# Middle projection ahead of the forward transform, 16-bit sine angles, merged product instructions, a partly moved bonus, free PSUM banks and a new written order in a two-layer RWKV-6 / Hyena kernel

## The chip, the cores and the metric

One core of one Trainium2 chip runs the whole program. The metric is device time in microseconds (us), the median of several executions. A profile of one execution accompanies it; its span is counted from the first to the last profiled event, and the time of an execution is a little longer than its span.

Five instruction queues work side by side, each strictly in its own order: PE (TensorE, matmuls; its weight loads are shown as PEld), DVE (VectorE), ACT (ScalarE), POOL (GpSimd) and SP (SyncE, which issues most DMA transfers). An instruction that waits for another queue holds up everything behind it in its own queue.

## The reference

Two layers follow one another. The first is a linear recurrence with a decaying state (batch 4, 8 heads, 768 steps, 48 wide); the second projects its output three ways, convolves the middle projection with a filter by a Fourier transform, gates it with the two others and projects it out.

```python
for t in range(S):
    cur = np.einsum('bhd,bhe->bhde', u[None] * kt, vt)
    y[:, :, t] = np.einsum('bhd,bhde->bhe', rt, state + cur)
    state = wt[:, :, :, None] * state + np.einsum('bhd,bhe->bhde', kt, vt)
...
x = attn_out.transpose(0, 2, 1, 3).reshape(B, S, H * D)
proj = x @ w_proj
x1, x2, x3 = (proj[..., :D], proj[..., D:2 * D], proj[..., 2 * D:])
X2 = np.fft.rfft(x2, n=S, axis=1)
H = np.fft.rfft(filter_fft, n=S, axis=0)[None, :, :]
x2_conv = np.fft.irfft(X2 * H, n=S, axis=1)
y = x1 * x2_conv * x3
return y @ w_out
```

Everything arrives and leaves in float32; matmuls run on bf16 operands. In the second layer the width is 384.

## The kernel before

**First layer.** The 768 steps of each batch are six chunks of 128, 24 chunks in all (0 to 5 are batch 0, and so on). Chunks are loaded in groups: {0}, {1}, {2, 3}, {4, 5} and then pairs. Every chunk has four loads of 192 KB (lw, lk, lr, lv), issued by SP. For a chunk the steps are, by the names in the written order:

- ln (ACT): logarithm of w; cs (PE): its running sums, as two 128x384 matmuls and four tiny ones; ex (ACT): exponentials; kq (DVE): k and r scaled by them; ph (ACT): the decay of the whole chunk.
- tr (PE) turns kq, qk (ACT or DVE) copies the turned tile out of PSUM, sc (PE) forms the 128x128 scores of eight heads, mt (DVE, or ACT followed by mc on POOL) masks them, half of the heads at a time.
- rk, ru, rh, cc (POOL and DVE) form the bonus r.(u*k), vb is v in bf16, vc (mostly POOL) is v times the bonus. yi (PE) adds vc into the chunk's output through an identity matmul of two 128x192 pieces.
- ki, kv (PE) and su (DVE) carry the state; ys (PE) applies it; y (PE) applies the masked scores; xn copies the output to SBUF; yt (PE) turns it and xT copies that.

**Second layer.** For each batch, `second(b)` describes:

- gates: p (PE) and cp (ACT or DVE) give x1; q and cq (DVE) multiply by x3. Together they need wproj0 and wproj2.
- the middle path: sd (DVE, POOL) folds the two halves of xn into sum and difference; z (PE) applies the forward transform table F to them; cz copies; f (PE) applies the middle projection; cf copies into X.
- products: U0 to U3 and P0, P1 multiply X by the filter's spectrum (HR, HI, HG).
- inverse: E (PE) with tables mi and mx, cE (ACT) copies one half, aE (DVE) adds and subtracts, dE (DVE, POOL) folds, yE multiplies by the gate; o (PE), co and so are the output projection, copy and store.

The filter's spectrum is made once, between (filt, fsd, h, hc, hg). The tables F, mi and mx are sines: DVE writes angles as 32-bit integers (ang, ia) and masks them to 16 bits (L1465, L1511), ACT takes the sine (sin, is0, is1). Sine, and the logarithm and exponential, need different activation tables; each change of table is a load on ACT.

**Order.** Nothing is scheduled automatically. A long string lists every step with its engine (P, A, D, G, S, or "-" for a step that is left out) and, for PE, the PSUM bank it writes; a trailing name ties a POOL step behind a DVE step. Each queue gets its instructions in exactly this order. `warm n b` puts n matmuls without a use into PE's queue. PSUM's eight banks are three pairs and two singles. k, r, v and w have three load slots each, one slot per group, so that group 3 reuses the slot of group 0.

Of the kernel before, what the change touches and what calls it, by code (L numbers as in the profile page):

```python
# [12 lines left out]
INT32 = mybir.dt.int32  # L13
AF = mybir.ActivationFunctionType
# [21 lines left out]
NLD, NG, NF, NS, NX, NO = 3, 2, 4, 3, 5, 5  # L36
NP = 3
# [4 lines left out]
smalls D  # L42
maps G
lw0 S
kz2 D
kz0 D
u S
kz3 D
kz1 D
xz D  # L50
lk0 S
imaps G
pads D
lr0 S
lv0 S
masks G
ur A
lw1 S
um P 3
lk1 S  # L60
ub A
lr1 S
ang0 D
lv1 S
vb0 A
ia2 D
lw2 S
sin0 A
ia1 D
lk2 S  # L70
ia0 D
lr2 S
lv2 S
iw D
vb1 A
ang2 D
lw3 S
is0 A
is1 A
lk3 S  # L80
ang1 D
sin2 A
lr3 S
rk0 D
lv3 S
sin1 A
rk1 D
ru0 D
table A
ru1 D  # L90
rh0 D
rh1 G ru1
cc0 D
vc0 G ru1
cc1 D
ln0 A
ln1 A
lw4 S
warm 27 1
cs0 P 0  # L100
vc1 D
cs1 P 1
rk2 D
ex0 A
ex1 A
kq0 D
vb2 G rk2
ln2 A
kq1 D
ru2 G rk2  # L110
lk4 S
warm 7 2
tr0 P 4
ph0 A
lr4 S
cs2 P 2
qk0 D
ph1 A
lv4 S
kv0 P 3  # L120
ex2 A
cs3 P 0
lw5 S
su0 D
rh2 G rk2
sc0 P 1
lk5 S
ex3 A
kq2 D
tr1 P 4  # L130
ki1 P 3
mt0.0 A
kv1 P
qk1 D
ph2 A
mt0.1 A
mc0.0 G rk2
tr2 P 2
lr5 S
kq3 D  # L140
sc1 P 1
mc0.1 G rk2
mt1.1 A
lv5 S
qk2 D
tr3 P 4
ph3 A
mt1.0 D
mc1.0 -
mc1.1 G rk2  # L150
yi0 P 0
qk3 A
y0 P
lw6 S
sc2 P 2
cc2 D
yi1 P 1
su1 D
ys1 P
mt2.1 A  # L160
lk6 S
vc2 G rk2
y1 P
xn0 D
ki2 P 4
ln3 A
kv2 P
mt2.0 D
mc2.0 -
sc3 P 0  # L170
lr6 S
yt0 P 3
xn1 A
su2 D
cs4 P 2
mt3.1 D
mc3.1 -
mc2.1 G rk2
xT0 A
yi2 P 1  # L180
lv6 S
ex4 A
ys2 P
mt3.0 D
mc3.0 -
rk3 G rk2
y2 P
yt1 P 4
ki3 P 3
xn2 A  # L190
xT1 D
cs5 P 0
lw7 S
kq4 D
yi3 P 1
yt2 P 4
ex5 A
kv3 P
lk7 S
vb3 G rk2  # L200
ys3 P
su3 D
y3 P
ph4 A
xT2 A
kq5 D
tr4 P 2
xn3 A
lr7 S
ki4 P 3  # L210
qk4 A
wproj0 G kq5
yt3 P 4
ru3 D
kv4 P
sd3.1 D
tr5 P 1
filt S
su4 D
xT3 A  # L220
rh3 G ru3
sc4 P 2
qk5 D
ph5 A
mt4.1 A
lv7 S
sd3.0 G ru3
cc3 D
warm 2 3
sc5 P 0  # L230
ln4 A
mt4.0 D
mc4.0 -
lw8 S
vc3 G ru3
mt5.1 D
mc5.1 -
warm 3 3
cs6 P 1
cs7 P 2  # L240
mt5.0 D
mc5.0 -
ex6 A
mc4.1 G ru3
yi4 P 0
ex7 A
kq6 D
ys4 P
y4 P
xn4 A  # L250
warm 2 4
tr6 P 3
ph6 A
sd4.1 D
lk8 S
sd4.0 D
yi5 P 0
yt4 P 4
qk6 A
kq7 D  # L260
rk4 G sd4.1
ys5 P
y5 P
lr8 S
p0.0.0 P 1
xT4 A
xn5 A
tr7 P 3
ph7 A
cp0.0.0 A  # L270
sd5.0 D
yt5 P 4
sd5.1 D
sc6 P 0
ru4 G sd5.0
xT5 D
qk7 A
p0.2.0 P 2
mt6.1 D
mc6.1 -  # L280
z0.2 P 1
mt6.0 D
mc6.0 -
cp0.2.0 A
rh4 D
p0.2.1 P 4
cz0.2 A
fsd0 D
lv8 S
sc7 P 2  # L290
z0.0 P 0
cp0.2.1 A
vb4 A
lw9 S
cc4 D
p0.0.1 P 1
cz0.0 A
fsd1 D
lk9 S
z0.1 P 0  # L300
cp0.0.1 A
lr9 S
mt7.1 D
mc7.1 -
wproj1 G fsd1
h0 P 1
cz0.1 A
mt7.0 D
mc7.0 -
lv9 S  # L310
vc4 G cc4
h1 P 2
hc0 A
lw10 S
ln5 A
kv6 P 3
hg0 D
h2 P 0
lk10 S
hc1 A  # L320
su6 D
ki7 P 4
yi6 P 1
hc2 A
y6 P
hg1 D
cs8 P 2
wproj2 G hg1
xn6 D
# [1486 lines left out]
```

## Time and profile before

| what | value |
|---|---|
| time, median of 3 runs | 159.8 us (159.7 to 160.09) |
| profiled execution, span | 159.0 us |
| HBM read, written | 22.41 MB, 4.72 MB |
| mean DMA rate over the span | 165 GB/s |
| load of w, k, r or v: 192 KB, issue to landing | 3.8 to 4.0 us (24 of each) |
| filter load, 1152 KB | 8.7 us |
| wproj loads, three of 288 KB (POOL queue) | 5.6 us |
| store of 384 KB / 192 KB | 2.7 / 1.9 us |

The span is shorter than the time by the launch and the end of the program. In the profile an "L" number is a line of the kernel; a helper's line (L1194 multiplies, L1198 and L1200 copies) stands for many steps, so steps are told apart by the tiles they write. "idle before" with an arrow names what ended the idle time of an engine. A slice of the page's second part is a fortieth of the span, and its digits are busy tenths. A window row gives busy time, with the number of instructions in brackets.

### The profile page before, as it was taken

What the parts mean: (1) busy time and instruction counts of PE and PEld (TensorE: products, weight loads), DVE (VectorE), ACT (ScalarE), POOL (GpSimd) and SP (SyncE); (2) the same over time, 40 slices, a digit from 0 to 9 for tenths busy, and PEclk for the clock granted to TensorE, in tenths of its full rate; (3) what the DMA queues carried; (4) which work ended last, traced back from release to release, by engine and by line L of the source; (5) the groups of instructions that cost most, each with busy time, mean ns of one, the idle gap of its engine ahead of it and who ended that gap; (6) DMA issues with size and microseconds to landing.
All of it is one profiled execution on the core that took longest, in us unless ns stands there. A gap on an engine that the chain in (4) does not pass through costs nothing.

```text
span 159.0 us, 4355 instructions
## 1 busy us (share of the span) xinstructions
PE 143.1 (90%) x1674; PEld 92.0 (58%) x1675; DVE 139.4 (88%) x289; ACT 126.6 (80%) x218; POOL 92.7 (58%) x98
## 2 busy tenths in 40 slices
PE   0990798998999999999999999999999999999880
PEld 0340366755656766757666777676677667666530
DVE  7992559988894999999999999999998999999980
ACT  4469848987889985999989989999988967775631
POOL 7411535976715166999957899879688823200400
PEclk9998579999999999999999999999999999999999
DMA  4999488999999999799998899989800004203136
GB/s 85 226 219 221 91 170 160 203 179 288 246 194 188 232 202 203 138 173 211 209 214 177 174 222 200 190 157 265 258 0 4 0 35 173 93 2 139 63 149 247
DMA packets 104118, 26.23 MB, mean 165 GB/s; under 512 B 100129, under 2 KB 102690, under 8 KB 104098
## 3 DMA queue, kind: packets, MB, share of 16 engines
q1 hardware_dynamic: 102498, 24.78, 70.4%
q0 software_dynamic: 1600, 1.18, 5.4%
q8 instruction: 13, 0.21, 0.6%
q14 instruction: 7, 0.06, 0.1%
HBM read 22.41 MB, written 4.72 MB: 171 GB/s over the span
## 4 chain that ended last, share of the span: by engine, by line
PE 61%; ACT 14%; DVE 12%; issue 4%; SPq 4%; DMA 2%; POOL 1%; ACTq 0%
PE pair L1573 8%; PE pair L1608 8%; PE pair L1626 6%; PE single L1333 5%; PE pair L1725 5%; PE pair L1345 3%; PE single L1573 3%; SPq L1278 3%; PE pair L1663 3%; PE pair L1420 3%; DMA v<-in_v_dram 2%; PE pair L1312 2%; PE single L1436 2%; PE pair L1403 2%; DVE U L1194 2%
## 5 line engine op out<-in xcount | busy, mean ns | idle before, releaser
L1321 DVE TENSOR_TENSOR kq<-pair,kr 128x768 bf16<-128x768 f32 x24 | 22.7, 952 | 2.2 <-ACT pair L1318 2.0
L1318 ACT ACTIVATE pair<-pair 128x768 f32<-128x768 f32 x24 | 19.3, 811 | 4.7 <-PE pair L1315 4.7
L1359 DVE TENSOR_TENSOR mt<-pair,mask_excl 128x512 bf16<-128x512 f32 x32 | 20.8, 682 | 0.3 <-PE pair L1345 0.2
L1573 PE MATMUL pair<-xT,wproj 128*128 128x384 bf16 x99 | 18.7, 326 | 0.0
L1194 POOL TENSOR_TENSOR vc<-vb,cc 128x768 bf16<-128x768 bf16 (+1 forms) x12 | 17.6, 1474 | 1.8 <-DVE cc L1297 1.1
L1573 PEld LDWEIGHTS <-wproj 128*128 128x128 bf16 x144 | 12.8, 97 | 7.3
L1194 POOL TENSOR_TENSOR rk<-kr 128x768 bf16<-128x768 f32 x8 | 15.2, 1905 | 3.0 <-DVE sd L1449 2.3
L1449 POOL TENSOR_TENSOR sd<-xn,xn 128x384 bf16<-128x384 bf16 x11 | 11.4, 1043 | 5.6 <-ACT xn L1198 4.2
L1363 POOL TENSOR_SCALAR_AFFINE_SELECT mt<-mt 128x512 bf16<-128x512 bf16 x16 | 11.6, 733 | 5.3 <-ACT phi L1325 3.9
L1697 POOL TENSOR_TENSOR y<-wv 128x384 bf16<-128x384 bf16 x6 | 5.6, 933 | 15.4 <-DVE wv L1691 12.1
L1294 POOL TENSOR_TENSOR rx<-rx 128x384 bf16<-128x384 bf16 (+1 forms) x7 | 6.9, 985 | 12.5 <-DVE rx L1194 12.4
L1333 PEld LDWEIGHTS <-kq 128*128 128x128 bf16 x192 | 12.1, 99 | 3.1 <-DVE kq L1321 1.0
L1198 ACT ACTIVATE o<-pair 128x768 f32<-128x768 f32 (+1 forms) x12 | 9.3, 783 | 5.7 <-PE pair L1725 5.7
L1198 ACT ACTIVATE qk<-single 128x1024 bf16<-128x1024 bf16 x13 | 13.4, 1032 | 0.5 <-PE single L1333 0.4
L1725 PE MATMUL pair<-wout,y 128*128 128x384 bf16 x69 | 13.4, 326 | 0.1
L1608 PE MATMUL pair<-F,sd 128*128 128x384 bf16 x72 | 13.2, 326 | 0.0
L1626 PE MATMUL pair<-wproj,Z 128*128 128x384 bf16 x72 | 13.0, 326 | 0.0
L1312 PE MATMUL pair<-lg,mask_neg 128*128 128x384 bf16 x24 | 8.1, 339 | 5.3 <-ACT lg L1284 5.2
L1333 PE MATMUL single<-ident,kq 128*128 128x128 bf16 x160 | 12.4, 223 | 0.1
L1198 ACT ACTIVATE xn<-pair 128x384 bf16<-128x384 f32 x22 | 10.8, 497 | 1.7 <-PE pair L1420 1.7
L1198 ACT ACTIVATE Z<-pair 128x768 bf16<-128x768 f32 x12 | 9.7, 815 | 2.1 <-PE pair L1608 2.1
L1229 PE MATMUL pair<-wt 128*128 128x512 bf16 x34 | 11.0, 495 | 0.0
(124 smaller groups left out, 381.1 us busy)
## 6 DMA issues: line engine op xcount, KB each, us to landing
w<-in_w_dram SPq DMA_DIRECT2D x24, 192.0 KB, 4.0
kr<-in_k_dram SPq DMA_DIRECT2D x24, 192.0 KB, 3.9
kr<-in_r_dram SPq DMA_DIRECT2D x24, 192.0 KB, 3.8
v<-in_v_dram SPq DMA_DIRECT2D x24, 192.0 KB, 3.8
out_dram<-o SPq DMA_DIRECT2D x11, 384.0 KB, 2.7
U<-in_moe_filter_fft_dram SPq DMA_DIRECT2D x1, 1152.0 KB, 8.7
wproj<-in_moe_w_proj_dram POOLq DMA_DIRECT2D x3, 288.0 KB, 5.6
out_dram<-o SPq DMA_DIRECT2D x2, 192.0 KB, 1.9
```

Of the source, the lines that this page charges most:

```text
L1194: return eng(e).tensor_mul(o, a, b)
L1198: return nc.scalar.activation(out=o, in_=a, func=AF.Copy)
L1318: op(f"ex{i}", [ACT], lambda e, bk: nc.scalar.activation(out=two(bk, f"cs{i}")[:, :, 0:C], in_=two(bk, f"cs{i}")[:, :, 0:C], func=AF.Exp), ...
L1321: op(f"kq{i}", [DVE], lambda e, bk: nc.vector.tensor_mul(kq[f][:, :, :, 0:D], two(bk, f"cs{i}")[:, :, 0:C].rearrange("p a (h d) -> p a h d ...
L1333: nc.tensor.transpose(p[:, HP * m + j, :], kq[f][:, m, 2 * j:2 * j + 2, :], ident)
L1359: return copy(e, o, x) if e == ACT else nc.vector.tensor_mul(o, x, _mid(mask_excl, HP))
L1363: return nc.gpsimd.affine_select(out=o, in_=o, pattern=[[0, HP], [1, L]], compare_op=ALU.is_gt, fill=0.0, base=0, channel_multiplier=-1,)
L1449: op(f"sd{i}.{z}", [DVE, POOL], lambda e, bk, z=z: eng(e).tensor_tensor(out=sd[:, ti, z, :], in0=lo, in1=hi, op=ALU.subtract if z else ALU ...
L1573: nc.tensor.matmul(p, wproj[:, cb, col0:col0 + L], xT[bx][:, cb, sl], start=(cb == 0), stop=(cb == CB - 1),)
L1608: nc.tensor.matmul(two(bk, n)[:, q, 0:HALF].rearrange("p (a f) -> p a f", a=2), sd[:, ti, q, cb * L:(cb + 1) * L], F[:, ti, :].rearrange(" ...
L1626: nc.tensor.matmul(two(bk, n)[:, z, 0:C], Z[:, cb, z, m * L:(m + 1) * L], wproj[:, cb, C:2 * C], start=(cb == 0), stop=(cb == CB - 1),)
L1725: nc.tensor.matmul(view(bk)[:, z], yt_[:, z, :], wout[:, cb, :], start=(cb == 0), stop=(cb == CB - 1),)
```

## The change

**Middle path.** x is now projected first: `side` (xw, PE) multiplies the turned chunks xT by the middle third of w_proj, cxw copies to x2, `fold` makes sum and difference of x2 (in batches 0 to 2 as one 128x1152 instruction each for sum and difference), and `fw` applies F to the folded x2. z, cz and the fold of xn are gone. The middle frequency block uses two column halves of 64, as the filter's transform does already.

```diff
-        def zz(cb):
-                for q in (0, 1):
-                    for ti in range(NT):
-                        nc.tensor.matmul(
-                            two(bk, n)[:, q, 0:HALF].rearrange("p (a f) -> p a f", a=2),
-                            sd[:, ti, q, cb * L:(cb + 1) * L],
-                            F[:, ti, :].rearrange("p (a g f) -> p a g f", a=2, g=2)[:, :, q, :],
+        def side(c0, n):
+                for z in range(n):
+                    for cb in range(CB):
+                        nc.tensor.matmul(
+                            view(bk)[:, z], xT[bx][:, cb, (c0 + z) * L:(c0 + z + 1) * L], wproj[:, cb, C:2 * C],
+        def fold(ti, n):
+                    out=sd[:, z, ti:ti + n], in0=x2[:, ti:ti + n], in1=x2[:, NT + ti:NT + ti + n],
         def fw(m):
-                    for cb in range(CB):
-                        nc.tensor.matmul(
-                            two(bk, n)[:, z, 0:C], Z[:, cb, z, m * L:(m + 1) * L], wproj[:, cb, C:2 * C],
+                    for z in (0, 1):
+                        fwd(two(bk, n)[:, z, 0:C], m, z, (sd[:, 0], sd[:, 1]), tis)
```

**Products and spectrum.** The four arrays of the spectrum are one tile hh (with one sign turned), so that two U instructions of twice the length and one P addition replace four and two. hc writes both parts in one instruction.

```diff
-                ("U0", U[:, 0, sl], X[:, 0, sl], HR[:, sl], None, "X", "H"),
...
+            for a in (0, 1):
+                op(f"u{a}{b}.{lo}", [DVE, POOL], lambda e, bk, a=a: mul(
+                    e, U[:, a, :, sl], _mid(X[:, a, sl], 2), hh[:, a, :, sl]),
+            op(f"p{b}.{lo}", [DVE], lambda e, bk: nc.vector.tensor_add(P[:, :, sl], U[:, 0, :, sl], U[:, 1, :, sl]),
```

**Inverse.** E may be written in two ways. With "Q" it is as before and dE folds afterwards (batches 1 and 2). With "P" all its matmuls are 384 wide, the tables hold both signs, and dE is left out (batches 0 and 3). The sign copies of the tables are made once by `flips` on POOL.

```diff
-                        o = at(bk, q) if m == 1 else at(bk, q)[:, QT * (m // 2):QT * (m // 2) + QT]
...
+                        o, x = at(bk, q), mi[:, m, q]
+                        if e == FOLD:
+                            o, x = (o, mx[:, q]) if m == 1 else (o[:, m // 2, :], mi[:, m, q, 0])
+                        elif m == 0:
+                            x = _mid(mi[:, 0, q, 0, :], 2)
+                        nc.tensor.matmul(o, P[:, q, m, cs], x, start=start, stop=stop)
```

**Bonus.** For chunks 6, 11, 12, 13, 16, 17 and 19 to 23 yi is left out; xn adds vc on DVE instead of being a copy.

```diff
+            if e == ADD:
+                return nc.vector.tensor_add(o, yview(bk), vcq.rearrange("p (j a) d -> p a j d", a=2))
             return copy(e, o, yview(bk))
```

**Masks.** mt and mc may take all eight heads in one 128x1024 instruction (engine letters M, N, C).

**Tables.** The angles are no longer masked: ACT reads the low 16 bits of each 32-bit word. One instruction takes the sines of the inverse tables. The trig table is loaded first on ACT, and the copies of u and v wait until after it; the u steps ur and ub are DVE's.

```diff
+        op("trig", [ACT], lambda e, bk: nc.scalar.preload_act_table_set("trig_and_small"), w=["trig"])
+        def turn(x):
+            return x.bitcast(UINT16).rearrange("p (c z) -> p c z", z=2)[:, :, 0]
...
-            nc.vector.tensor_scalar(
-                out=d, in0=d, scalar1=int(UNIT) - 1, scalar2=None, op0=ALU.bitwise_and,
-            )
```

**Slots, banks, warm-up.** k, r and v have four slots, lg, rk and vc three, xn three; rx is gone (ru and rh write over rk). PSUM is one tile of eight banks and a pair is any two neighbouring banks. Warm-up is 30 matmuls of 256 columns at the start, and none later (before: 27 of 512 at the start, 15 of 512 later).

```diff
-NLD, NG, NF, NS, NX, NO = 3, 2, 4, 3, 5, 5
-NP = 3
+NLW, NLD, NG, NF, NS, NX, NO = 3, 4, 3, 4, 3, 3, 5
-    banks = [ps.tile([L, 2, 512], FP32, name=f"pair{i}") for i in range(NP)]
-    banks += [ps.tile([L, 1, 512], FP32, name=f"single{i}") for i in range(8 - 2 * NP)]
+    banks = ps.tile([L, 8, 512], FP32, name="banks")
```

**Order.** The whole list is written anew. Its beginning, read as queues: SP loads w0, r0, k0, k1, w1, u, w2, w3, r1, r2, k3, r3, k2, v0, v2, v1, w4, w5, v3, k4, r4, r5, k5, v4, v5, w7, w6, k7, k6, r6, r7, the filter, v7. ACT has the trig table, sin2, sin1, sin0, is, the table of the logarithm, ln1, ln0, ln2, then the exponentials of chunks 1, 0, 3 and 2. POOL has the maps, ia0, the masks (tied to ang0), then rk0, rk1. DVE has ang2, ang1, ang0, ia2, ia1, ur, ub. On PE the first chunk steps are cs1, cs0, cs3, cs2, tr1, tr0, tr3; xw0.2 and xw0.0 stand ahead of y4 and y5.

## The prediction

> **What bounds the kernel now.** First the page's busy shares and slices.
>
> ```profile
> PE 143.1 (90%) x1674; PEld 92.0 (58%) x1675; DVE 139.4 (88%) x289; ACT 126.6 (80%) x218; POOL 92.7 (58%) x98
> PE   0990798998999999999999999999999999999880
> DVE  7992559988894999999999999999998999999980
> ACT  4469848987889985999989989999988967775631
> PEclk9998579999999999999999999999999999999999
> ```
>
> A slice is 4 us. From the eleventh on PE stands at 9. Its two 9s at 4 to 12 us are 27 warm-up matmuls (L1229), which compute nothing. The timeline shows what real work waits for.
>
> ```profile
> 8.53 0.94 ACT L1491 ACTIVATE F<-o,mpi 128x768 bf16<-128x768 int32 x1
> 10.66 0.52 ACT L1198 ACTIVATE vb<-v 128x384 bf16<-128x384 f32 x1 [1.20 <-DMA v<-in_v_dram]
> 11.09 0.92 ACT L1516 ACTIVATE mi<-U,mpi 128x768 bf16<-128x768 int32 x1
> 13.15 1.76 ACT L1491 ACTIVATE F<-o,mpi 128x768 bf16<-128x768 int32 x2
> 14.92 1.28 ACT L1530 ACT_TABLE_LOAD   x1
> 16.78 0.48 PE L1312 MATMUL pair<-lg,mask_neg 128*128 128x384 bf16 x1 [4.56 <-ACT lg L1284]
> ...
> 39.80 0.37 PE L1420 MATMUL pair<-vb,mt 128*128 128x48 bf16 x8
> ```
>
> Start and length in us stand first. ACT's queue is in order: the sine tables stand behind copies that wait for v, the logarithm behind the sines and a table load, and the first real matmul (cs0) starts at 16.78. The last line is y5, the end of chunk 5. I cut the span there, and at y11, y17, y23 and PE's end:
>
> ```profile
> 16.80:40.00 23.20, 21.76 (x324) 14.24 (x325) 19.26 (x33) 17.56 (x34) 15.26 (x16) 0.89 0.88 185
> 40.00:74.00 34.00, 33.31 (x416) 21.70 (x413) 30.24 (x52) 30.39 (x56) 21.68 (x21) 1.00 1.05 197
> 74.00:106.10 32.10, 31.85 (x440) 21.90 (x437) 31.01 (x61) 30.19 (x54) 27.84 (x22) 1.00 0.97 192
> 106.10:131.30 25.20, 25.20 (x337) 17.51 (x334) 24.46 (x46) 21.55 (x39) 17.86 (x16) 1.00 0.38 101
> 131.30:154.60 23.30, 22.50 (x154) 13.41 (x150) 22.45 (x61) 14.95 (x23) 3.95 (x4) 1.00 0.26 99
> ```
>
> Columns are the window's length, busy us of PE, PEld, DVE, ACT, POOL, and the granted clock. From 40 us PE is busy 112.9 of 114.6 us and DVE 108.2. So there are three parts: a start bound by loads and ACT's queue (40.0), a body where PE bounds and DVE follows closely (114.6), and 4.4 of output.
>
> **The change, part by part: the body.** The chain of waits prices PE work: six 128x384 matmuls 0.98 (0.163 each), a 128x192 half of that (0.082).
> - Middle projection. Before, a batch's path z, f is 18 + 18 matmuls. Now it is 18 for xw and 24 for f, of which 12 write 64 columns. The filter's own 12 of that form (L1475) run from 48.50 to 49.50, as long as six full ones: 36 by price, as before. If such halves don't overlap, each batch pays 0.98 more (3.9 in all). I take 0. On ACT or DVE a copy of x2 takes the place of Z's (0.815). The fold was 24 instructions of 128x384, 11 of them on POOL at 1043 ns. For three batches it is now six of 128x1152 on DVE, 0.764 by the P row: POOL loses 10.4 (only one fold is left there), DVE exchanges 13 x 0.353 = 4.6 for 6 x 0.764 + 5 x 0.353 = 6.3.
> - Inverse. In batches 0 and 3 the signs go into PE's operand: 24 matmuls grow from 192 to 384, +24 x 0.082 = +2.0. In return 12 folds of y (0.359 on DVE, 0.933 on POOL) disappear, half of them in the tail.
> - Bonus. For 11 chunks its two 128x192 matmuls go: -22 x 0.082 = -1.8. Their xn leaves ACT (0.497) for DVE as an addition. No such form is shown. Bounds: 0.35 (bf16 from SBUF) and 0.95 (768 from PSUM); I take 0.55, the wv row, of the same size from PSUM. DVE +6.1. Such an xn now waits in DVE's queue behind kq or mt, and yt, xT and the projections wait for it.
> - Merged products. U: six of 128x2304 for 12 of 1152. Bounds 0.764 and 3 x 0.764; the slope from 384 (0.349) to 1152 (0.76) gives 1.39: DVE 8.3 for 9.1. P: 1.39 for 2 x 0.764. The last batch has 6 + 3 instructions of 768 at 0.574 for 12 + 6 of 0.349: 5.2 for 6.3, in the tail.
> - Masks of 1024. DVE between 0.95 and 2 x 0.682; by slope 1.22, 8 of them. ACT between 0.85 and 2 x 0.613; I take 1.03, the qk row. POOL's cut between 0.733 and twice that; 1.2. Together -1.2 on DVE, -1.2 on ACT.
> - Banks free. Any two neighbouring banks make a pair. No bank reuse shows as a long wait before; I take 0, between -2 and +2, which is about the 1.7 us that PE idles in the body.
> - xT, qk and some copies change engine by the new order: DVE +4, ACT -4.
>
> By these prices PE's work behind y5 is 109.6 before and 109.4 now (the new order does two xw, 1.96, ahead of y5 where the old one did cs6, cs7 and tr6, 1.45). DVE's instructions behind y5 sum to 115.0 and 116.0 by mean durations less 35 ns of overlap each, 1% more, so some 109 busy. ACT loses 6. POOL stays at 71 against 70, but 31.5 of it now lies between y11 and y17, where PE has 29.9. The body before took 114.6 - 109.6 = 5.0 more than PE's prices; I keep that: 109.4 + 5.0 = 114.4.
>
> **The start.** One masking instruction less per angle table (L1465, 0.56) and the L1511 one (0.80): ACT reads the low 16 bits instead. A sine from them isn't shown; bounds 0.81 (a plain copy of 768) and twice 0.93; I take 0.93, and for the merged 1152 1.25 by slope.
> The trig load opens ACT's queue (0.80 to 2.08). maps ends at 2.3 as before; DVE's clears (wt, smalls, pads, two kz) end at about 2.5, and three angle groups at 0.9 give 3.4, 4.3, 5.2. POOL's ia0 ends near 5.0, DVE's ia2 and ia1 at 6.4. Sines end at 4.3, 5.2, 6.1, the merged one at 7.7; the table load at 9.0, ln1 at 9.5, and cs1 runs there. masks (2.4 on POOL, tied to ang0) end at 7.5. ur and ub, now on DVE behind ia1, end by 8, ahead of ru0's operands.
> Then the loads bind. In the timeline SP issues about every 0.85 us from the fourth, and a load lands 3.9 after its issue (DMA part of the page). r1 is now ninth: issue 6.7, lands 10.7. ex1 ends at 11.6, kq1 at 12.6 (kq0 before: 19.4). k2, thirteenth, lands at 14.3, v0, fourteenth, at 15.1. vb0 waits for it at the head of ACT's queue, with mt0.1, mt1.1, qk3, qk2 behind it; y0 comes near 18. v3, nineteenth, lands at 19.3, r5 and k5 at about 22, v5 at 24.4. The fourth slot of k, r, v lets all of chunks 0 to 5 come without waiting for kq0, as group 3 did (SP idle from 14.5 to 16.8 and 17.1 to 19.5). ACT then runs ln3, vb2, xn1, ex4 to 23.2, DVE kq4 to 24.1, and POOL's queue is the last: vc2 to 24, rk3 (1.9) to 26, vb3, mc4.1 to 27.5, vc3 to 29.5, mc4.0 to 30.2, and y4, y5 follow. POOL issues wproj1 at 22, ahead of rk3, and wproj0 after 30; that lands 5.6 later, at 36, behind 4.5 us of PE work (cs6, cs7, yt, xw, tr, f): cover, at most 1 us short. The filter's load stands thirty-first on SP, issues near 26 and lands 8.7 later, with v6 and v7 behind it; the filter's matmuls come after the gates that wait for wproj0.
> So y5 comes at about 31.0 instead of 40.0. A replay by hand misses small waits; its bounds are 28.5 (v5 landed, then 4 us of queue) and 34.
>
> The removed fill of 15 warm matmuls (7 of them at 18.3 to 21.4) is where the trace speaks against it. After 4.6 idle us PE ran at granted 0.50 (16 to 20 us) and 0.78 (20 to 24). The new start has a like gap after its 30 shorter warm-ups, then sparse matmuls. In the Trainium skill, "TensorE: Matmul & The Clock Gate", "Part 1: The HAM clock gate", full clock comes after a window of about 3.4 us of sustained work. The gap agrees with the 0.50 here; how dense the work must be no run here shows.
>
> **Sum.** 31.0 + 114.4 + 4.4 = 149.8 span; the last store is now a 192 KB one (1.9 against 2.7 us, its copy 0.56 against 0.81): -0.4. The median of the runs is 159.8 for a span of 159.0, so +0.8: 150.2.
>
> **Rivals.**
> A. Half clock through the sparse start. A chunk's path has cs, tr, sc, y: 0.50 + 0.45 + 0.33 + 0.25; doubled for the two chunks that follow one another, +3.1: 153.3. For it the 0.50; against it that the loads, not PE, set the pace there.
> B. DVE turns the body over. Each of the 11 xn additions holds PE for one more DVE instruction ahead of it, kq's 0.952: +10.5, 160.7. It decides from 0.92 us each. For it: DVE is busy 31.01 of 32.1 us from 74 us on. Against: in the new order several PE steps lie between most y and their yt (kv, tr, E and sc behind y11).
> C. The body shrinks too: ACT's 6 us less and free banks give back PE's 5.0 of waits, 3.5 of them: 146.7. Against: DVE's 109 us remain.
> D. The move gives no full gain: halves of f that don't overlap, +3.9: 154.1. The L1475 row speaks against it.
>
> **How the numbers follow.** Chances: forecast 0.60, A 0.14, B 0.07, C 0.11, D 0.08. The forecast's own range is 147.5 to 153 (y5 from 28.5 to 34 in full). With A, C and D, 146 to 156.5; B and a double mishap stay outside. About 0.3% (0.5 us) can be told from no change: faster 0.92, within 0.01, slower 0.07, which is B.
>
> **What would show it.** The first real matmul near 9.5 us and y5 near 31; PE at 9 from the ninth slice on; f's halves with 12 in about 1 us; U of 2304 near 1.39, the 1024 mask near 1.22, the addition near 0.55; body 114. Wrong if y5 comes after 35, or if PE's idle time in the body, named after DVE, passes 8 us.

## The result and the profile after

The changed kernel takes 167.8 us (median of 4 runs, 166.5 to 168.9), the kernel before 159.9 on the same chip: ratio 1.048, 95% interval 1.0415 to 1.0546. The forecast was 150.2, with 156.5 as its upper end. The profiled execution took 167.7 us for a span of 165.9. Here and below a ratio leaves out executions over 1.5% longer than the fastest of their kernel, so it need not be the quotient of two medians, and where too few are left none is formed.

These are the changed kernel's lines of busy time and slices (a slice is now 4.15 us):

```profile
PE 144.2 (87%) x1665; PEld 94.9 (57%) x1665; DVE 140.3 (85%) x259; ACT 117.7 (71%) x192; POOL 99.3 (60%) x103
PE   7868877984984999649999999999989999999980
DVE  6758999892799889375899999999999999999950
PEclk9965999998699599965999999999999999999997
```

PE's busy total is nearly what it was (143.1 before). But where the old kernel showed an unbroken row of 9s from the eleventh slice on, PE now dips in slices 10, 13 and 17 to 18, and the granted clock dips right behind each, in 11, 14 and 18 to 19. The start, by the timeline (start and length in us first):

```profile
3.41 2.62 ACT L1453 ACTIVATE F<-o,mpi 128x768 bf16<-128x768 uint16 x3 [1.35 <-DVE o L1427]
6.34 1.25 ACT L1453 ACTIVATE mi<-U,mpi 128x1152 bf16<-128x1152 uint16 x1 [0.30 <-DVE U L1465]
...
9.48 0.32 PE L1278 MATMUL banks<-lg,mask_neg 128*128 128x384 bf16 x1 [1.64 <-ACT lg L1250]
...
31.32 0.57 PE L1389 MATMUL banks<-vb,mt 128*128 128x48 bf16 x16
```

The sines come first, the first real matmul starts at 9.48 (16.78 before) and y5, the end of chunk 5's output, comes 8.3 us earlier than before (31.9 against 40.2; the cuts, here and in the prediction, lie some 0.2 ahead of that end, at 31.7 and 40.0). Cut as before at y5, y11, y17, y23 and PE's end (window's length, busy us of PE, PEld, DVE, ACT, POOL, granted clock, DMA share, GB/s):

```profile
0.00:31.70 31.70, 25.24 (x330) 18.42 (x331) 25.34 (x67) 23.53 (x38) 25.09 (x45) 0.89 0.98 189
31.70:83.50 51.80, 42.07 (x464) 26.77 (x461) 39.43 (x60) 31.65 (x52) 26.13 (x22) 0.87 1.03 204
83.50:114.20 30.70, 30.68 (x418) 20.44 (x413) 30.25 (x51) 27.18 (x45) 26.44 (x21) 1.00 0.83 159
114.20:137.70 23.50, 22.86 (x320) 15.57 (x316) 23.43 (x40) 19.50 (x33) 15.95 (x12) 1.00 0.14 52
137.70:161.00 23.30, 23.30 (x162) 13.72 (x158) 21.27 (x45) 15.25 (x26) 5.72 (x6) 1.00 0.25 96
```

The start is 8.3 us shorter. Of the last three windows the first two are 1.4 and 1.7 us shorter and the third is as long as before. All of the loss is in one window: y5 to y11 takes 51.8 us where it took 34. There PE is idle for 9.7 us, and the granted clock is 0.87 in the mean, because it falls to half ("half clock" from here on) for some stretches. A finer cut of that window shows three pairs, an idle stretch and a slow one behind it:

```profile
37.60:39.75 2.15, 0.03 (x2) 0.01 (x1) 0.37 (x1) 1.73 (x2) 0.28 (x1) 1.00 1.13 241
39.75:44.00 4.25, 4.25 (x17) 2.10 (x17) 1.99 (x4) 0.00 (x0) 1.87 (x2) 0.61 0.92 177
50.70:53.30 2.60, 0.18 (x9) 0.10 (x4) 2.60 (x3) 0.81 (x2) 2.05 (x2) 1.00 1.06 172
53.30:57.50 4.20, 3.85 (x52) 2.94 (x52) 3.60 (x10) 2.22 (x4) 0.00 (x0) 0.62 1.16 206
69.20:72.85 3.65, 0.04 (x2) 0.01 (x1) 1.49 (x3) 0.03 (x1) 2.98 (x4) 0.80 1.12 223
72.85:78.50 5.65, 5.65 (x49) 3.69 (x50) 3.59 (x5) 3.32 (x6) 4.03 (x4) 0.53 1.11 216
```

What each stall waits for is read from the timeline of the same stretch:

```profile
30.78 0.88 SPq L1495 DMA_DIRECT2D U<-in_moe_filter_fft_dram  x1
31.08 0.80 POOL L1227 DMA_DIRECT2D wproj<-in_moe_w_proj_dram  x1
...
39.75 3.18 PE L1536 MATMUL banks<-xT,wproj 128*128 128x384 bf16 x12 [2.12 <-DMA wproj<-in_moe_w_proj_dram]
...
48.66 1.52 POOL L1158 TENSOR_TENSOR vc<-vb,cc 128x768 bf16<-128x768 bf16 x1 [5.91 <-DVE cc L1263]
48.77 1.53 DVE L1514 TENSOR_SCALAR hh<-hh 128x384 bf16<-128x384 bf16 x1
...
50.39 2.51 DVE L1514 TENSOR_SCALAR hh<-hh 128x384 bf16<-128x384 bf16 x1
50.96 1.81 POOL L1158 TENSOR_TENSOR rk<-kr 128x768 bf16<-128x768 f32 x1
...
53.22 0.26 PE L1389 MATMUL banks<-vb,mt 128*128 128x48 bf16 x4 [2.42 <-DVE S L1362]
...
53.96 0.26 DVE L1514 TENSOR_SCALAR hh<-hh 128x384 bf16<-128x384 bf16 x1
...
64.73 1.25 POOL L1482 TENSOR_SCALAR mi<-mi,sgn 128x384 bf16<-128x384 bf16 x1
65.97 2.45 POOL L1484 TENSOR_SCALAR mx<-mi,sgn 128x384 bf16<-128x384 bf16 x2
68.40 1.16 POOL L1486 TENSOR_SCALAR mi<-mi 128x384 bf16<-128x384 bf16 x1
69.53 1.79 POOL L1158 TENSOR_TENSOR rk<-kr 128x768 bf16<-128x768 f32 x1
...
72.84 1.89 PE L1299 MATMUL banks<-ident,kq 128*128 128x128 bf16 x16 [3.61 <-DVE kq L1287]
```

First stall: SP issues the filter's 1152 KB at 30.78, POOL issues wproj0 at 31.08, and wproj0 lands 8.6 us later, at 39.7. Second: DVE's negated copy of hh (L1514) takes 0.26 us when GpSimd is idle, at 53.96. Its two earlier ones take 1.53 and 2.51 and end as POOL's vc and rk end (50.2 and 52.8); S and chunk 6's output wait behind them. The longer of the two starts 0.57 us ahead of rk, while POOL is issuing a load of w_proj (50.13 to 50.94), so rk alone doesn't account for its first part. In the kernel before, DVE's three copies of this size took 0.25 to 0.26 us each, the last two beside an idle POOL:

```profile
50.80 0.26 DVE L1550 COPY HG<-HR 128x384 bf16<-128x384 bf16 x1
```

Third: the four instructions of `flips` hold POOL for 4.8 us ahead of rk6, and ru6, kq10 and PE's transposes wait in a row.

### The profile page after: what moved, and what is told of

The parts are those of the page before. It is cut to its first block, busy times and chain, and to the rows that moved or that the text cites. A ratio compares the mean times of both kernels' runs of the same rounds, so it can differ in the third digit from the quotient of the medians.

```text
span 165.9 us, 4290 instructions
## 1 busy us (share of the span) xinstructions
PE 144.2 (87%) x1665; PEld 94.9 (57%) x1665; DVE 140.3 (85%) x259; ACT 117.7 (71%) x192; POOL 99.3 (60%) x103
## 4 chain that ended last, share of the span: by engine, by line
PE 29%; DVE 22%; POOL 15%; DMA 12%; issue 11%; ACT 7%; SPq 1%; POOLq 0%; ACTq 0%; DVEq 0%
PE banks L1536 6%; POOL rk L1158 6%; DMA wproj<-in_moe_w_proj_dram 5%; PE banks L1438 5%; PE banks L1299 4%; DMA out_dram<-o 3%; PE banks L1692 3%; PE banks L1573 3%; POOL mt L1332 3%; DVE kq L1287 3%; PE banks L1628 2%; DVE hh L1514 2%; DMA w<-in_w_dram 2%; DMA kr<-in_k_dram 2%; POOL vc L1158 2%
## 5 line engine op out<-in xcount | busy, mean ns | idle before, releaser
L1536 PE MATMUL banks<-xT,wproj 128*128 128x384 bf16 x144 | 29.8, 344 | 2.7 <-DMA wproj<-in_moe_w_proj_dram 2.1
L1332 POOL TENSOR_SCALAR_AFFINE_SELECT mt<-mt 128x512 bf16<-128x512 bf16 (+1 forms) x17 | 15.9, 937 | 16.5 <-ACT mt L1162 11.8
L1287 DVE TENSOR_TENSOR kq<-banks,kr 128x768 bf16<-128x768 f32 x24 | 22.7, 950 | 2.2 <-ACT banks L1284 1.9
L1162 ACT ACTIVATE x<-banks 128x768 bf16<-128x768 f32 (+1 forms) x26 | 18.0, 700 | 6.1 <-PE banks L1573 4.0
L1158 POOL TENSOR_TENSOR rk<-kr 128x768 bf16<-128x768 f32 (+1 forms) x12 | 20.1, 1679 | 2.6 <-DMA kr<-in_r_dram 1.3
L1299 PE MATMUL banks<-ident,kq 128*128 128x128 bf16 x192 | 16.8, 243 | 5.1 <-DVE kq L1287 4.5
L1284 ACT ACTIVATE banks<-banks 128x768 f32<-128x768 f32 x24 | 19.1, 804 | 0.5 <-PE banks L1281 0.2
L1327 DVE TENSOR_TENSOR mt<-banks,mask_excl 128x512 bf16<-128x512 f32 (+1 forms) x17 | 15.6, 934 | 2.4 <-PE banks L1311 2.0
L1162 ACT ACTIVATE qk<-banks 128x1024 bf16<-128x1024 bf16 x14 | 14.1, 1028 | 2.4 <-PE banks L1299 2.3
L1438 PE MATMUL banks<-sd,F 128*128 128x384 bf16 (+1 forms) x96 | 14.0, 336 | 0.3 <-DVE sd L1584 0.3
```

The source lines that it names most:

```text
L1158: return eng(e).tensor_mul(o, a, b)
L1162: return nc.scalar.activation(out=o, in_=a, func=AF.Copy)
L1284: op(f"ex{i}", [ACT], lambda e, bk: nc.scalar.activation(out=two(bk, f"cs{i}")[:, :, 0:C], in_=two(bk, f"cs{i}")[:, :, 0:C], func=AF.Exp), ...
L1287: op(f"kq{i}", [DVE], lambda e, bk: nc.vector.tensor_mul(kq[f][:, :, :, 0:D], two(bk, f"cs{i}")[:, :, 0:C].rearrange("p a (h d) -> p a h d ...
L1299: nc.tensor.transpose(p[:, HP * m + j, :], kq[f][:, m, 2 * j:2 * j + 2, :], ident)
L1327: return copy(ACT, o, x) if e in (ACT, ACT2) else nc.vector.tensor_mul(o, x, _mid(mask_excl, z - HP * a))
```

## The experiments

Chips differ here. The kernel before had a median of 163 us on all the chips that the experiments ran on, against 160 in its first profile, so only ratios, and stages within a trace, are set side by side. "Profiled" is the time of the one execution that the trace shows. For each trace I took the window from y5 to y11 and split it: idle time of PE, half-clock loss (over windows of 1 us, busy time times one minus the granted clock), and the rest, work at full clock. A later y5 shortens the wait for wproj0 in this window without any edit to it: in e1 y5 comes 4.2 us later than in the first profile and the load's issue only 2.1, and the wait is 0.3 us.

| run | profiled | y5 | y5 to y11 | work | idle | half clock | median | ratio, 95% interval |
|---|---|---|---|---|---|---|---|---|
| before, first profile |  | 40.0 | 33.9 | 33.2 | 0.7 | 0 | 159.9 | |
| after, first profile | 167.7 | 31.7 | 51.8 | 36.0 | 9.7 | 6.0 | 167.8 | 1.048 (1.0415 to 1.0546) |
| c_before | 164.4 | 40.5 | 33.9 | 33.2 | 0.7 | 0 | 162.9 | 0.999 (0.9946 to 1.0039) |
| c_after | 172.2 | 34.1 | 54.0 | 36.2 | 10.4 | 7.4 | 169.4 | 1.0245 (1.0176 to 1.0314) |
| e1 flips early | 163.8 | 35.9 | 44.4 | 36.1 | 5.3 | 3.0 | 163.8 | none formed |
| e2 sign from PSUM | 169.3 | 35.5 | 49.4 | 36.3 | 9.0 | 4.1 | 167.1 | 1.0208 (1.0135 to 1.028) |
| e3 wproj0 early | 169.0 | 37.4 | 47.5 | 35.8 | 8.4 | 3.3 | 168.6 | 1.0327 (1.0261 to 1.0394) |
| e4 the three together | 162.9 | 36.6 | 42.8 | 36.8 | 4.3 | 1.7 | 164.6 | 1.0041 (0.9975 to 1.0107) |
| e5 hh on ScalarE | 165.7 | 32.9 | 48.6 | 36.8 | 8.4 | 3.4 | 166.3 | 1.0156 (1.0109 to 1.0202) |
| e6 e5 + flips early | 160.4 | 34.1 | 42.8 | 37.1 | 5.7 | 0 | 162.0 | 0.9872 (0.9802 to 0.9941) |
| e7 e6 + filter later | 161.6 | 35.0 | 43.5 | 36.3 | 4.0 | 3.2 | 161.8 | 0.9881 (0.9813 to 0.9949) |
| e9 stalls filled | 166.4 | 35.6 | 47.3 | 36.8 | 2.6 | 0 | 166.4 | 1.0193 (1.0084 to 1.0303) |
| e13 stalls filled, other banks | 163.6 | 32.9 | 47.3 | 36.8 | 2.6 | 0 | 165.8 | 1.0082 (1.0025 to 1.0139) |
| e11 e6 + start filled | 162.7 | 34.8 | 42.2 | 37.1 | 5.1 | 0 | 161.0 | 0.9858 (0.982 to 0.9896) |
| e12 e11 + filter, wproj1 later | 164.8 | 33.4 | 46.3 | 38.6 | 4.7 | 3.0 | 166.7 | 1.0154 (1.0055 to 1.0253) |
| e14 all three away, rest filled | 163.0 | 34.0 | 41.2 | 37.1 | 2.0 | 0 | 161.6 | 0.9859 (0.9794 to 0.9924) |
| e15 e14 + start filled | 163.6 | 35.3 | 44.5 | 36.9 | 3.8 | 1.7 | 163.7 | none formed |

In e9 and e13 filler of 7.9 us, in e14 and e15 of some 2, is taken out of the work column. That column hardly moves, 36 to 37 us in nearly every run (e12 moves two projections of 0.98 us in); what moves is idle time and clock.

**The controls.** Both kernels, unedited.

> The changed kernel itself, unedited, as the control of this set of four: the earlier four runs came from a chip on which the kernel before took 163.5 us, so totals of the two sets can't be set side by side. Theory (three stalls between the end of chunk 5's and chunk 11's output matmuls, y5 to y11: wproj0 beside the filter's load, the sign instruction held by GpSimd, the flips ahead of rk6): y5 to y11 takes 50 to 53 us, ratio to before 1.035 to 1.06. Whether y5 ends at 31 to 32 us (start as in the first profile of this kernel) or at 35 to 37 (as in all four experiments so far) tells whether those experiments' later start came from the chip or from their edits.

The three stalls came back in the same places: 3.1 us for wproj0, 2.4 for S, 3.6 for kq, and 54.0 us from y5 to y11, in one row:

```profile
34.10:88.10 54.00, 43.56 (x464) 27.28 (x461) 39.50 (x60) 31.68 (x52) 25.90 (x22) 0.84 0.96 192
```

The window was 1 us longer than I had expected, and the ratio, 1.0245, lies below my 1.035: the loss here is about half of that in the first profile, where the kernel before was 3 us faster. y5 at 34.1 lies between the two answers that I had offered; in the runs that change nothing ahead of it y5 lay between 32.9 and 35.9.

> The kernel before, unedited, profiled on the same chip as the three others of this set. Theory (what makes it 163 us here and 160 in its first profile is a longer spell of half clock in its start): half-clock loss ahead of y5 over 4 us (2.5 in the first profile), y5 at 41.5 to 44, y5 to y11 33.5 to 34.5 as in the first profile, with under 1.5 us idle. Rival (this chip's loads or engines are slower throughout): y5 to y11 or y11 to y23 over 1 us longer than in the first profile.

My theory fell. The half clock ahead of y5 was 1.6 us, y5 came at 40.5 and y5 to y11 took 33.9, as in the first profile. What got longer was y11 to y17: 35.2 us against 32.1, with ACT waiting 2.0 us for loads of w, and POOL 2.0 and DVE 1.0 for loads of r. So in an execution on these chips loads can land too late in that stage, in the old kernel too.

**The flips.** They move to the place where POOL stood idle for 7.6 us (from 31.9 to 39.5).

```diff
 wproj0 G
+if G
...
-if G
 rk6 G rh5
```

> The changed kernel, with the four sign copies (flips, 4.8 us on POOL) moved from ahead of rk6 into POOL's idle stretch at 32 to 39 us. Theory 1 (the loss is three stalls of batch 0, each followed by a stretch of half clock): PE's 3.6 us wait before tr10 at 69 to 73 us goes, and the half clock of 72 to 78 us with it (PE busy 5.2 us there at 0.5: 2.6): about 162 us instead of 167.8. Theory 2 (DVE and the new order are simply too full in the body, a removed wait comes back at the next step): under 1 us, 167 or more.

The wait on kq10 and its half clock were gone, the wait on S (2.5 us) and the half clock behind that remained; y5 to y11 took 44.4. Not all of that is the flips' doing: y5 came 4 us later than in the first profile, and PE then waited only 0.3 us for wproj0. No ratio could be formed; the four runs took 160.1 to 164.3 us, those of the kernel before 160.7 to 164.5.

**The sign.** In e2 the negated copy is read from PSUM:

```diff
+nc.vector.tensor_scalar(
+    out=hh[:, 1, 0, n, :], in0=two(bk, f"h{n}")[:, 1, 0:C], scalar1=scl0 if n == 0 else 2.0 / S,
+    scalar2=-1.0, op0=ALU.mult, op1=ALU.mult)
...
-nc.vector.tensor_scalar(
-    out=hh[:, 1, 0, n, :], in0=hh[:, 0, 1, n, :], scalar1=-1.0, scalar2=None, op0=ALU.mult)
```

> The changed kernel, with the sign-turned part of the spectrum made from PSUM instead of from the SBUF copy (same values; three instructions expected at 0.55 each instead of 1.53, 2.51, 0.26). Theory 1 (the two long ones stood still for as long as POOL's vc and rk ran): PE's 2.4 us wait at 50.8 to 53.2 and part of the half clock of 54 to 58 us (1.5) go: about 164 us. Theory 2: under 1 us. A third theory for these lines, that the instruction is slow by itself: its PSUM form would be long too, over 1 us each.

In e2 (and e4) chunk 6's state matmuls overwrite h2's bank ahead of that read, so part of hh isn't the filter's spectrum. The trace tells more than the time. DVE, hh alone:

```profile
50.16 0.26 DVE L1510 COPY hh<-hh 128x384 bf16<-128x384 bf16 x1
50.33 0.55 DVE L1511 TENSOR_SCALAR hh<-banks 128x384 bf16<-128x384 f32 x1
...
52.52 1.95 DVE L1510 COPY hh<-hh 128x384 bf16<-128x384 bf16 x1
```

From PSUM the negated copy (L1511) takes 0.55 to 0.60 us each time, so it isn't slow by itself. The hold went over to the plain copy that still goes from SBUF to SBUF (L1510: 0.26 free, 1.95 held, as long as rk runs): moving one of two such instructions out of POOL's way gives little, and the ratio, 1.0208, can't be told from the control's. So e5 moves both.

```diff
+nc.scalar.activation(out=hh[:, 1, 1, n, :], in_=p[:, 0], func=AF.Copy, scale=2.0 / S if n else scl0)
+nc.scalar.activation(out=hh[:, 1, 0, n, :], in_=p[:, 1], func=AF.Copy, scale=-2.0 / S if n else scl0n)
...
-nc.vector.tensor_copy(out=hh[:, 1, 1, n, :], in_=hh[:, 0, 0, n, :])
...
-out=hh[:, 1, 0, n, :], in0=hh[:, 0, 1, n, :], scalar1=-1.0, scalar2=None, op0=ALU.mult)
```

> Of the filter's spectrum, the copy and the negated copy that VectorE made from SBUF (hg, L1510 and L1514) are made by ScalarE from PSUM, six more ScalarE instructions of some 0.4 us; nothing else differs. Theory (a VectorE copy or multiply from SBUF to SBUF is held while GpSimd's vc and rk run): the wait of the output matmuls of chunk 6 on DVE S falls from 2.4 us to under 0.6 and y5 to y11 gets 2.5 to 4.5 us shorter than in the control, time 2.5 to 4.5 us less. Rival (VectorE simply had too much ahead of S): the wait stays over 1.5 us and the time within 1 us of the control.

PE no longer waits for S. It now waits 1.1 us for ScalarE's last copy, which keeps kv6's bank. y5 to y11 fell by 5.4 us against the control, 0.9 of it a shorter wait for wproj0, and by 3.2 against the first profile. In both comparisons some 1 us is a shorter spell of half clock behind the third stall, which e5 doesn't touch. By ratio the gain is 0.9 points (1.0245 to 1.0156), and the two intervals overlap.

> The edit of the run before, and the flips behind wproj0's issue in GpSimd's order, where GpSimd stood idle for 7.6 us, instead of ahead of rk6. Theory: PE's wait on kq of chunk 10 falls from 3.6 us to under 0.7 and the half clock behind it goes; y5 to y11 43 to 46 us, time 5.5 to 8.5 us under the control, ratio to before 0.985 to 1.01. Rival (PE is held by VectorE's sum of work in this stage and the waits only move): y5 to y11 over 47.5 us.

As the theory had it: 42.8 us from y5 to y11, no half clock in it, and the first version that beats the kernel before, though by 1.3% only.

```profile
34.10:76.90 42.80, 37.15 (x462) 24.20 (x459) 35.07 (x54) 33.83 (x58) 25.75 (x22) 1.00 1.01 204
```

PE's wait on kq10 fell from 3.5 us (e5) to 0.4. Of the 5.8 us between e5 and e6 some 2.2 lie at the first stall, whose wait was 0.5 shorter and had no half clock behind it; neither is the flips' doing.

**wproj0 and the filter.** Two ways to the same load: issue wproj0 earlier, or the filter later.

```diff
 wproj1 G
+wproj0 G
...
-wproj0 G
```

> The changed kernel, with the load of the first third of w_proj issued on POOL right behind that of the second (near 22.7 instead of 31 us). Theory 1: it no longer shares the DMA engines with the filter's 1152 KB (8.6 us to landing, 5.6 before the change); PE's wait of 2.1 us up to 39.75 goes and the half clock of 40 to 44 us (1.7): about 164 us, less up to 1 us that the issue costs on POOL ahead of vc2. Theory 2: under 1 us.

PE no longer waited for wproj0. But with 288 KB more beside the loads of chunks 4 and 5, PE waited 4.75 us for POOL's cast of v and did nothing from 28 to 32 us; y5 came at 37.4, and at 36.6 in e4, which has the same edit, against 35.9 and 35.5 in e1 and e2 on that chip. The expected 164 us didn't come (168.6). In e1, e2 and e4 the wait for that cast was 2.0 to 2.8 us, so how much of the 4.75 is the edit's stays open. The other two stalls remained.

```diff
-filt S
...
 lv6 S
+filt S
```

> As the run before, and the filter's 1152 KB load is issued behind lv6 instead of behind xw0.0's copy, some 3 us later, so that wproj0 (288 KB) has less beside it. Theory: wproj0 lands 5.5 to 7 us after its issue instead of 8.6, PE's wait ahead of the middle projection (2.1 us) falls under 0.7, the time 1 to 3 us under the run before. Rival (the 16 DMA engines are full, what comes earlier for one load comes later for another): PE waits instead for P (made from the filter), 1.5 us or more, and the time is within 1 us of the run before or longer.

Issued 1.5 us ahead of the filter, wproj0 lands 6.0 us after its issue instead of 8.5 in e6, and PE doesn't wait for it. How long the load takes goes with which of the two issues ends first. In ten traces that of wproj0 ends last, and it lands 8.0 to 9.6 us after its start; in e7, e12, e14 and both traces of the kernel before it ends first, and it lands in 5.1 to 6.0 (e3 and e4 issue it some 10 us earlier). Yet PE's waits in e7, from y5 to y11, name another instruction (us in total, times, longest):

```profile
PE banks L1441 <- DVE P L1501: 1.6, 1, 1.6
PE banks L1355 <- ACT hh L1511: 1.1, 1, 1.1
```

The rival held: same time as e6. Some 0.6 us of the wait for P is DVE and POOL holding each other up again: P's two additions take 3.24 us instead of 2.61, beside a cast of v on POOL.

**The half clock.** Dummy matmuls ahead of each stall keep PE busy and take nothing off another engine. In e9 those ahead of y6 went into bank 1, which chunk 8's scan still needed, so its data were not numbers; e13 repeats it with banks that the next matmul overwrites.

```diff
+warm 20 4
 p0.2.1 P 4
...
+warm 20 1
 cs8 P 0
...
+warm 30 3
 tr10 P 3
```

> The changed kernel with dummy matmuls (128x256 on the constant tile, results overwritten) on PE ahead of its three stalls: 20 ahead of the middle projection, 20 ahead of chunk 6's output, 30 ahead of chunk 10's transposes; nothing is taken off any other engine. Theory (each stall costs twice: the idle time itself, 9.8 us from y5 to y11, and half clock behind it, 6.0 us in the first profile of the changed kernel and 7.4 in the control, because PE stood idle): the waits for wproj0, S and kq stay in place behind the filler, the granted clock stays at 1.0 from y5 to y11, and the time falls by 4 to 7 us under the control, ratio to before 0.985 to 1.015. Rival (the half clock comes with the amount of work and not with the idle time): the clock still falls to 0.5 for some us in each of the three places and the time stays within 1.5 us of the control.

> The changed kernel with dummy matmuls (128x256 on the constant tile) ahead of its three stalls: 20 ahead of the middle projection, 20 ahead of chunk 8's scan (the last work before chunk 6's output), 30 ahead of chunk 10's transposes, each into a bank that the matmul behind it overwrites. Theory (half clock follows idle time of PE): waits for wproj0, S and kq remain behind the filler, granted clock 1.0 from y5 to y11, y5 to y11 46 to 49 us (51.9 and 54.0 without the filler), ratio to before 1.00 to 1.02. Rival (the half clock in the earlier filler run was away because its data were no numbers, or comes with the work itself): clock at 0.5 for 3 us or more behind at least two of the stalls, y5 to y11 50 us or more.

e13, the window from y5 to y11 and two lines of its PE timeline:

```profile
32.90:80.20 47.30, 44.66 (x531) 31.04 (x528) 39.16 (x60) 31.63 (x52) 25.92 (x21) 1.00 1.01 201
```

```profile
38.58 2.35 PE L1196 MATMUL banks<-wt 128*128 128x256 bf16 x20
40.76 2.11 PE L1539 MATMUL banks<-xT,wproj 128*128 128x384 bf16 x12
```

The clock is 1.00 throughout, and 12 matmuls behind the first stall take 2.11 us where they took 3.18. Nothing that PE waited for came sooner, and y5 to y11 is 4.5 us shorter than in the first profile of the changed kernel and 6.7 shorter than in the control. So the half clock is a consequence of the stalls, and costs another 60 to 70% of PE's idle time (6.0 to 9.7 in the first profile, 7.4 to 10.4 in the control). By ratio the gain is smaller, 1.6 points (1.0245 to 1.0082), and e9's, at 1.0193, stayed above the 1.015 that I had expected at most.

**What is left.** The start:

```diff
 um P 0
+warm 14 7
...
+warm 8 7
 cs4 P 2
```

> The copies of hh on ScalarE and the flips early, as before, and dummy matmuls in two gaps of the start: 14 behind um (ahead of the first scan), 8 ahead of chunk 4's scan. Theory (the later y5 of 34 to 37 us in these runs is half clock in the start, 4.6 us of it in the run without the filler): half-clock loss ahead of y5 under 1.5 us, y5 at 30 to 32.5, time 2 to 4 us under that run, 158 to 160, ratio to before 0.963 to 0.98. Rival (the start waits for its loads): y5 stays at 33.5 or later and the time within 1 us of 162.

> As the run before, and the filler in two gaps of the start. Theory (y5 of 33 to 35 us in these runs is half clock in the start): y5 at 31 to 32.5, time 1 to 2.5 us under the run before. Rival (loads that land late set y5): half clock ahead of y5 under 2 us, yet y5 at 33.5 or later with PE waiting for v's cast or the scan's logarithm, and time within 0.7 us of the run before.

y5 came late in both, as the rival had it (e15's time, 163.7, lay above the rival's range too). The half-clock loss of the first 34 us was 4.6 in e6 and 1.5 (e11) and 1.7 (e15) with the filler, but y5 stayed at 34.8 and 35.3. Yet these two runs don't show that the loads set y5, because the filler ahead of cs4 did harm of its own. In e11:

```profile
21.86 1.87 PE L1196 MATMUL banks<-wt 128*128 128x256 bf16 x8 [1.45 <-ACT xn L1165]
```

It waited for xn1 to leave the bank that it writes, and held PE's queue: cs4, whose logarithm was there at 20.6, started at 23.5 (21.5 in e6). In e15 it waited 1.76 us. A better witness is e14, which has no filler there, lost nothing to half clock ahead of y5, and still had y5 at 34.0; POOL and DVE each waited 0.8 us for a load of k and ACT 0.6 for one of w. So in that execution the clock is not what held y5, and loads had a part in it.

e12, beside e11's edits and e7's:

```diff
-wproj1 G
...
 vb3 G su3
+wproj1 G
...
-xw0.2 P 3
...
-xw0.0 P 0
...
 xT5 D
+xw0.2 P 1
+cxw0.2 A
+xw0.0 P 4
+cxw0.0 D
```

> As the run before, the filter's load behind lv6, and the two fill projections xw0.2 and xw0.0 behind y5 with wproj1's load issued behind vb3's cast instead of behind mc3.1, some 5 us later, so that chunk 4's and 5's v are loaded without it. Theory (loads share the queues' 200 GB/s, and 288 KB out of the way is some 1.4 us): y5 1 to 2 us earlier than in the run before, no wait for wproj0, wait for P 1 to 2 us; time 0 to 2 us under the run before. Rival (the sum of what must be loaded stays, so a wait for wproj1 or wproj0 takes its place): y5 earlier, but PE waits 1.5 us or more for a DMA between y5 and h1, time equal or longer.

e12 keeps e11's filler in the start. Here xw0.2 takes a bank of chunk 6's scan, so its data are wrong from there on. y5 came 1.4 us earlier than in e11, but PE waited 2.7 us for POOL, whose queue now held wproj1's issue ahead of vc: inconclusive for the loads, worse in time.

e4 joins the edits of e1, e2 and e3. e14 joins those of e7 (with e5's and e1's) and fills two waits that remain; e15 adds e11's filler.

```diff
+warm 12 0
 h1 P 0
...
+warm 8 1
 kv6 P 3
```

> All three edits together. Theory 1: the stalls (2.1 + 2.4 + 3.6) and their half clock (5.9) go: 154 us, the time from y5 to y11 falls from 51.9 to about 38. Theory 2: 164 us or more, with new waits of the same length in the same stretch.

> Copies of hh on ScalarE, flips early, filter's load behind lv6, and dummy matmuls, 12 ahead of h1 (where PE waits for P) and 8 ahead of chunk 6's state matmuls (where PE waits for hh). Theory (the three stalls and their half clock are the whole miss of the body): y5 to y11 39 to 42 us with no half clock, of which 37 are work and 2 filler or waits; ratio to before 0.965 to 0.985. Rival (loads set the pace of chunks 6 to 11): y5 to y11 over 43 us with waits for loaded tiles (kr, v, w) of 2 us or more.

In e4 y5 to y11 came down to 42.8 instead of the expected 38, and the time to 164.6 instead of 154: PE still waited 1.6 us for P and 1.3 for S, and y5 came at 36.6. e14 takes all three stalls away: y5 to y11 took 41.2 with 2.0 us idle, about 39 without the filler. But the time is e6's, and its ratio too. In e15, with the same edits and the start's filler, SP reached the filter's load 0.4 us ahead of POOL's wproj0, which took 8.8 us to land, and PE waited 2.0 us for it. Lines of e14 for a later stretch of the profiled execution:

```profile
101.55 0.82 POOL L1167 CAST vb<-v 128x768 bf16<-128x768 f32 x1 [4.29 <-DMA v<-in_v_dram]
102.43 0.31 PE L1357 MATMUL banks<-vb,kq 128*64 128x48 bf16 x8 [2.82 <-POOL vb L1167]
```

```profile
100.00:104.00 4.00, 1.57 (x30) 1.09 (x29) 1.51 (x4) 0.83 (x1) 2.45 (x3) 0.99 0.92 179
104.00:108.00 4.00, 3.96 (x34) 1.93 (x33) 1.97 (x3) 1.73 (x3) 4.00 (x4) 0.58 1.10 219
```

POOL waits 4.3 us for a load of v, PE 2.8 for POOL, and the clock falls behind that. y11 to y17 took 35.0 where the changed kernel, slower up to there, took 30.7. DMA is full in that stretch (its share near 1, 176 to 202 GB/s from 84 to 104 us); by SP's order the later of that cast's two loads was issued at 94.8, and it landed 6.7 us later. In this execution what was gained by y11 is given back to the loads by y17, as in c_before's; e11's trace has the like (33.9, POOL waiting 3.8 us for a load of v) and e12's less of it (32.5), while in e6, e7 and e15 the stage took 30.7. e14's execution took 2.8 us more than the shortest of its runs (160.2), so the wait need not be in every run; in the shorter ones it can't be seen what limits.

## Why the prediction was wrong

In the first profile the miss of 17.5 us (167.7 against 150.2) splits, by the forecast's own sum: start 31.7 for 31.0, +0.7; body 129.3 for 114.4, +14.9; end of PE to end of span 4.9 for 4.0, +0.9; outside the span 1.8 for 0.8, +1.0. So the sign was lost in the body.

**Right.** The start, in its order and its size: first matmul 9.5, y0 at 17.9, y5 at 31.7 inside 28.5 to 34. That y5 is the earliest of all traces; with nothing changed ahead of it the others had it at 32.9 to 35.9, on chips where the kernel before was 3 us slower too, so the close hit is in part luck. Nearly every price of the body; by operation and shape:

```profile
L1327 DVE TENSOR_TENSOR mt<-banks,mask_excl 128x1024 bf16<-128x1024 f32 x8 | 9.7, 1218 | 0.4 <-ACT x L1162 0.4
L1158 DVE TENSOR_TENSOR U<-X,hh 128x2304 bf16<-128x2304 bf16 x6 | 8.1, 1351 | 0.0
L1401 DVE TENSOR_TENSOR xn<-banks,vc 128x384 bf16<-128x384 f32 x11 | 6.0, 553 | 0.1
L1438 PE MATMUL banks<-sd,F 128*64 128x384 bf16 x48 | 4.7, 330 | 0.0
```

Forecast 1.22, 1.39 and 0.55; measured 1.218, 1.351 and 0.553. The halves of f overlap: the 48 matmuls that write 64 columns sum to 4.7 us, 48 full ones to 9.4 (rival D out). So the work was right: from y5 on PE is busy 118.9 us, less 6.0 of half clock 112.9; the forecast had 112.7 (109.4 + 5.0, less 1.7 of idle time).

**Wrong, and the step.** "The body before took 114.6 - 109.6 = 5.0 more than PE's prices; I keep that." That carried 1.7 us of idle time over into a new order. The idle time was 10.4, and 6.0 of half clock came with it: +14.7 of the 14.9. Three things were not placed on the queues that they stand in:

- "wproj0 after 30; that lands 5.6 later, at 36, behind 4.5 us of PE work (cs6, cs7, yt, xw, tr, f): cover, at most 1 us short." The issue time was right (31.1). The landing was 8.6 because the filter's load, put at 26, was issued at 30.8, just ahead of it (e7 shows the difference). Stall 2.1, on the chip of the control 3.1.
- The sum of DVE's work has hg's instructions neither priced nor put beside POOL's vc and rk. By e5 they cost about 2.2 us of the window, idle time and clock together: 3.2 against the first profile, less the 1.0 at the third stall; 5.4 against the control, less 1.1 there and 2.1 at the first stall. That is net of the 1.1 us that PE then waits for ScalarE.
- The flips were named in the change and never put into POOL's queue. "31.5 of it now lies between y11 and y17" looked at a later stage. 4.8 us ahead of rk6 made 3.6 of wait; e6 against e5 shows 5.8 us of the window, some 3.6 without what lies at the first stall.

**The rivals.** A put 3.1 us of half clock into the start, and that much was lost there (10 to 17 us). y5 came on time all the same: either waits for loads hid the loss, or the replay by hand, which had no half clock in its sum, was too long elsewhere; no run shows which. The mechanism returned in the body, behind stalls, at twice the size. The page "TensorE: Matmul & The Clock Gate" of the Trainium skill, "Part 1: The HAM clock gate", has the clock fall after an idle window of about 3.4 us. Here it fell behind gaps of 2.1 and 2.4 us, and 2.1 us into the one of 3.6, so a gap shorter than that window was enough. B, the slower side, named the right engine for a wrong reason: PE's waits on xn sum to 0.3 us; DVE held PE as something that was itself held. C is out (no idle time given back).

Of "what would show it wrong", y5 held in the first profile (in e1, e2 and e9 it passed 35), and the mark of 8 us of PE idle after DVE came close, 3.9 + 2.4 + 0.5 + 0.3 + 0.3 = 7.4, but two of the three causes stood behind DVE: POOL's flips, and POOL holding up DVE's copies. The mark was blind to them, and to DMA.

The three stalls are not the whole miss. In e6, without the second and third and with no half clock between y5 and y11, the profiled execution (160.4) still lies 10.2 us over the forecast, on a chip where the kernel before took 163.4: y5 at 34.1 instead of 31.0, a body of 119.8 instead of 114.4 with 6.0 us of PE idle in it instead of 1.7, and another 1.8 behind PE's end and outside the span.

Open: what sets the loads' pace, whether it alone kept e14 from being faster than e6, why y5 varies from 31.7 to 35.9 in runs whose work ahead of it is the same, and what another order of the loads would give; none was tried beyond e3, e7 and e12. A start filled with matmuls that wait for nothing wasn't tried either.

## What to carry to other kernels

Wait times don't carry over with a new order: when a schedule is rewritten, put every added instruction, small ones too, into its engine's queue and read who stands behind it, on POOL above all. A PE stall over 2 us should be priced with the half clock behind it (here 1.5 to 2.7 us behind stalls of 2.1 to 3.6), and dummy matmuls in the gap take that second part away, if the bank that they write is free by then. Before summing a gain, ask what else is full: here loads kept DMA busy for some 100 us, and in the profiled run of e14 what PE saved by chunk 11 it waited for by chunk 17.

## What the hardware showed that I had not expected

DVE and GpSimd hold each other up by form of operand. A DVE multiply or copy of 128x384 from SBUF to SBUF went from 0.26 us to 1.53, 1.95 or 2.51 beside vc and rk; the same sign from PSUM stayed at 0.55 to 0.60. The Trainium skill has this in "SBUF — State Buffer", "Who interferes with whom": the pair of ports that both engines share is locked for a whole instruction, by copies and tensor_scalars that run in a two-port mode, and by two SBUF inputs against a GpSimd read. The trace agrees with the second case too: in e7 POOL's cast of v took 2.02 us beside P, against 0.82 in e6 where it ran ahead of P. What holds the 2.51 us instruction in its first 0.57 us, beside POOL's issue of a load, stays open; a copy just ahead of it ran beside that same issue in 0.25.

The clock keeps to a fixed grid. In every trace its spells at 0.5 within PE's work last 3.41 or 6.83 us, and they begin whole multiples of 3.41 us apart: at 9.93, 40.65, 54.30 and 71.37 in the first profile. So it goes by how much PE does in a stretch of that grid rather than by the length of one gap. In the first profile PE was busy 1.28, 1.08 and 1.27 us of the 3.41 ahead of the three spells of the body. Over all traces, from 33 to 153 us, all sixteen full-clock stretches in which it was busy under 1.7 us were followed by half clock, and none in which it was busy over 2.3; between the two it went either way. From y5 to y11 e6 stayed at full clock with gaps of up to 1.7 us, and e7's clock fell behind gaps of 1.6 and 1.1 us that lie 4 us apart. Where a stall falls on the grid differs between executions of one kernel (the first spell starts at 9.93 in the first profile, at 11.29 in c_after), so the half clock behind a stall is in part chance.
